# Linear attention and an MLP mixer in one kernel: attention on quarters of the PE array, u summed onto x in PSUM, pair 0 scaled in another order

## The chip, the cores and the metric

The kernel runs on one NeuronCore of a Trainium2 chip. Its engines work from queues of their own: TensorE (PE; its weight loads are listed as PEld), VectorE (DVE), ScalarE (ACT), GpSimd (POOL) and SyncE (SP), which issues most of the DMAs. The metric is the device time of one execution in microseconds. A profile's span is a little shorter than that time: 811.9 against 813.68 us for the profiled execution.

## The reference

Everything is float32. q, k, v have the shape (8, 8, 576, 64): batch, heads, sequence, head dimension.

```python
kv = np.einsum('bhsd,bhse->bhde', k, v)
out = np.einsum('bhsd,bhde->bhse', q, kv)
rms = np.sqrt(np.mean(out * out, axis=-1, keepdims=True) + 1e-06)
x = (out / rms * g_norm)                       # then (B, S, H*D) = (8, 576, 512)
h = np.maximum(x.transpose(0, 2, 1) @ w_tok1, 0.0) @ w_tok2
u = x + h.transpose(0, 2, 1)
out = u + np.maximum(u @ w_ch1, 0.0) @ w_ch2
```

w_tok1 is 576 x 256, w_tok2 256 x 576, w_ch1 512 x 1536, w_ch2 1536 x 512; the four weights arrive in 64 bits and are rounded to 32 by the kernel.

## The kernel before

There are two passes. The second (from 204.85 us on) computes the channel mixing with a Strassen scheme and is not touched. The first makes u for all eight batches and stores it to DRAM. It works on four pairs of batches; in a pair, "side" is the batch. 576 tokens are four blocks of 128 and a rest of 64, and the rests of both sides share one block, so a pair has nine blocks of x (0 to 8), held in tiles X of two blocks: chunk c of 0 to 3 is two blocks of one side, chunk 4 the rest.

The steps of a pair have short names, and the order of all engines' work is written out by hand as lists of these names (`start` for the first pair's attention, `middle`, `steady` twice, `last`). `play` runs the list, and every instruction keeps its program order on its engine. A number n in a list puts n steps of the rounding of w_ch1 and w_ch2 there (one on ACT, six on DVE a block). The mixing of pair n runs together with the attention of pair n + 1.

- `kv` s h: half h (four heads) of k^T v for side s, 20 matmuls of 128 rows by 64 columns, the two heads of a pair of heads going to the two column halves of the array. They write the diagonal blocks of `kv_ps[half]`, one of two PSUM tiles that were zeroed at the start (line 1010).
- `e` s h: the eviction to `kvp[side]`, 128 x 256 with the zero blocks in it; on DVE in pair 0, on ACT afterwards.
- `a` c t: attention for 128 tokens and all heads: four matmuls (`attend`, line 355), one for each pair of heads, into one bank of `ps["o"]`, which has two. Each matmul is two records in the trace[...].
- `g`, `q`, `t` c t: gain (DVE: x = out * g), square (ACT) and total (DVE: mean square by head). `m`, `r`, `i`: mean, square root (ACT) and inverse for a group of chunks.
- `s` c t: scaling of x by the inverse, eight ACT instructions (line 424); `p` c t: the same as one POOL instruction (line 428).
- `h` s t and `hr`: the first token product, 128 x 512 outputs in the four banks of `ps["h"]`, then four relus on ACT. In pair 0 `h01` is cut by blocks (`h010` to `h013`).
- `u` i: the second token product for block i into a bank of `ps["h"]`, then on DVE (line 480) the sum with x, which is stored with every second block.
- `l`, `lq`: the loads of k, v and q on SP's queue; `j` n: n matmuls of an identity, before the first data come.

In the lists, `e00` of a steady pair stands behind `s30` and `s31` of the list before:

```python
"u6 t30 t31 m2 r2 1 i2 p20 p21 s30", f"u7 1 s31 {n1}", "u8 2"]        # a steady list ends
"kv00 l00 e00 1 -s40", "h00 3", "kv01 l01 e01 1", "h01 3", ...        # the next begins
```

`-s40` is a step of the pair before. [...]two banks for `o`, four for `h`, and two tiles for `kv`.

## Time and profile before

| what | us |
|---|---|
| median of 3 runs (813.6 to 814.11) | 813.75 |
| profiled execution, its span | 811.9 |
| first pass, start to last token product | 204.85 |
| PE busy, whole span | 796.3 |
| DVE busy | 690.8 |
| ACT busy | 288.2 |
| POOL busy | 79.9 |

Busy time is a union over instructions: 98% for PE says that it nearly always had something in flight, not that a stage couldn't be shorter. A row of the groups reads: line, engine, operation, output<-inputs, shapes, count, then busy us and mean ns of one, then the idle time before them and what ended it. In the timeline the columns are start, length, engine and instruction, with idle time before it in brackets.

### The profile page before, as it was taken

Reading aid. Unit: us, or ns where it says so; the run is one execution under the profiler, and the core shown is the slowest. Engines: PE = TensorE matmul, PEld = TensorE weight load, DVE = VectorE, ACT = ScalarE, POOL = GpSimd, SP = SyncE. Lnnn points to the kernel's source line nnn. Section 1 sums busy time; section 2 is a strip of 40 time slices with the busy share of each in tenths; the row PEclk is TensorE's granted clock in tenths of the full one; section 3 lists DMA queues with packets and bytes.
Section 4 is the critical chain, followed back from the end, with each engine's and each line's share of the span. In section 5 each row is a group of like instructions: output and inputs, shape, how many; then the busy total and the mean of one; then the engine's idle time right before and its main releaser. Section 6 shows DMA issues by size and latency. Waiting matters only on the chain.

```text
span 811.9 us, 16377 instructions
## 1 busy us (share of the span) xinstructions
PE 796.3 (98%) x6388; PEld 704.9 (87%) x6388; DVE 690.8 (85%) x1318; ACT 288.2 (35%) x805; POOL 79.9 (10%) x75
## 2 busy tenths in 40 slices
PE   6999999999999999999999999999999999999997
PEld 6655565543888899999999999999999999999996
DVE  4688989999986978988997997897898899799687
ACT  1355566471120134243234233333424323423331
POOL 1210101010000011003003003001100200300300
PEclk9999999999999999999999999999999999999999
DMA  9999998335458477368558638737836855764642
GB/s 294 324 342 329 341 357 290 131 130 169 166 203 294 169 213 244 131 210 256 174 182 247 211 134 270 238 118 249 268 123 213 249 178 190 239 199 136 202 147 82
DMA packets 97341, 175.43 MB, mean 216 GB/s; under 512 B 7024, under 2 KB 54128, under 8 KB 97264
## 3 DMA queue, kind: packets, MB, share of 16 engines
q1 hardware_dynamic: 95584, 172.65, 65.4%
q10 hardware_dynamic: 1680, 1.74, 0.7%
q8 instruction: 50, 0.82, 0.4%
q14 instruction: 27, 0.22, 0.1%
HBM read 137.79 MB, written 36.57 MB: 215 GB/s over the span
## 4 chain that ended last, share of the span: by engine, by line
PE 88%; DVE 7%; DMA 3%; issue 1%; ACT 0%; SPq 0%; ACTq 0%; DVEq 0%
PE ps_a L127 37%; PE ps_b L127 18%; PE ps_c L127 9%; PE ps_u L127 5%; PE ps_h L127 5%; PE ps_v L127 4%; PE ps_w L127 4%; PE ps_o L127 2%; DMA v_in<-in_v_dram 2%; PE ps_kv L127 2%; DMA k_in<-in_k_dram 1%; DVE w_ch L174 1%; DVE ms L399 1%; DVE w_ch L118 1%; DVE part L187 1%
## 5 line engine op out<-in xcount | busy, mean ns | idle before, releaser
L118 POOL TENSOR_TENSOR v<-v,v 128x384 f32<-128x384 f32 (+1 forms) x48 | 61.4, 1301 | 534.0 <-ACT v L124 494.0
L124 ACT COPY u<-ps_a 128x128 f32<-128x128 f32 (+1 forms) x160 | 56.1, 351 | 156.9 <-PE ps_a L127 156.9
L127 PE MATMUL ps_b<-uT,sums 128*128 128x128 f32 x672 | 86.2, 276 | 0.0
L127 PEld LDWEIGHTS ps_b<-uT,sums 128*128 128x128 f32 x672 | 80.7, 192 | 0.2
L118 DVE TENSOR_TENSOR v<-v,v 128x768 f32<-128x768 f32 (+1 forms) x86 | 79.4, 930 | 1.1
L127 PE MATMUL ps_a<-uT,w_ch 128*128 128x128 f32 x576 | 78.9, 275 | 0.0
L124 ACT COPY ps_c<-ps_a 128x128 f32<-128x128 f32 (+1 forms) x80 | 26.9, 336 | 130.1 <-PE ps_a L127 130.1
L118 DVE TENSOR_TENSOR v<-ps_b,u 128x384 f32<-128x384 f32 x112 | 61.4, 548 | 12.8 <-PE ps_b L127 11.0
L127 PEld LDWEIGHTS ps_a<-uT,w_ch 128*128 128x128 f32 x576 | 71.5, 192 | 0.4
L127 PE MATMUL ps_u<-h,w_tok 128*128 128x512 f32 (+1 forms) x160 | 66.9, 602 | 0.5 <-DVE x L118 0.5
L127 PE MATMUL ps_h<-x,w_tok 128*128 128x512 f32 (+1 forms) x160 | 65.8, 603 | 0.0
L118 DVE TENSOR_TENSOR uT<-uT 128x512 f32<-128x512 f32 (+4 forms) x103 | 63.0, 628 | 0.8
L127 PE MATMUL ps_a<-uT,w 128*128 128x128 f32 x432 | 60.0, 275 | 0.0
L127 PEld LDWEIGHTS ps_a<-uT,w 128*128 128x128 f32 x432 | 54.0, 192 | 0.0
L127 PEld LDWEIGHTS ps_h<-x,w_tok 128*128 128x128 f32 (+1 forms) x160 | 25.9, 189 | 31.1 <-issue 28.3
L118 DVE TENSOR_TENSOR xg<-xg,r 128x512 f32<-128x512 f32 (+1 forms) x78 | 50.8, 663 | 2.3 <-ACT r L124 1.6
L127 PEld LDWEIGHTS ps_u<-h,w_tok 128*128 128x128 f32 (+1 forms) x160 | 24.7, 179 | 30.2 <-issue 22.6
L121 ACT ACTIVATE v<-v 128x384 f32<-128x384 f32 (+1 forms) x86 | 42.6, 528 | 22.8 <-DVE v L118 22.4
L118 DVE TENSOR_TENSOR sv<-v 128x384 f32<-128x384 f32 x80 | 43.3, 549 | 8.4 <-ACT v L121 8.4
L424 ACT ACTIVATE x<-x,inv 128x64 f32<-128x64 f32 x184 | 46.0, 335 | 9.5 <-DVE inv L419 8.1
L127 PE MATMUL ps_a<-sums,sv 128*128 128x128 f32 x336 | 47.0, 276 | 0.0
L127 PE MATMUL ps_a<-uT,sums 128*128 128x128 f32 x336 | 46.8, 276 | 0.0
(128 smaller groups left out, 1589.2 us busy)
## 6 DMA issues: line engine op xcount, KB each, us to landing
sums<-sums SPq DMA_DIRECT2D x112, 576.0 KB, 4.2
qT<-in_q_dram SPq DMA_DIRECT2D x8, 1152.0 KB, 10.1
xt<-u_dram SPq DMA_DIRECT2D x36, 256.0 KB, 3.5
blocks<-y SPq DMA_DIRECT2D x72, 128.0 KB, 2.6
uT<-blocks SPq DMA_DIRECT2D x36, 256.0 KB, 5.2
xg<-u_dram SPq DMA_DIRECT2D x18, 512.0 KB, 4.9
k_in<-in_k_dram SPq DMA_DIRECT2D x16, 512.0 KB, 9.4
u_dram<-x SPq DMA_DIRECT2D x16, 512.0 KB, 3.9
```

The costliest lines, as they stand in the source:

```text
L118: keep(engine.tensor_tensor(out=o, in0=a, in1=b, op=op))
L121: keep(nc.scalar.activation(o, a, AF.Relu))
L124: keep(nc.scalar.copy(o, a))
L127: keep(nc.tensor.matmul(*a, **kw))
L174: keep(nc.vector.scalar_tensor_tensor(out=bits, in0=raw()[..., 1], scalar=0x80000000, in1=bits, op0=ALU.bitwise_and, op1=ALU.bitwise_or))
L187: keep(nc.vector.scalar_tensor_tensor(out=part[0], in0=raw()[..., 0], scalar=2.0 ** -52, in1=part[0], op0=ALU.mult, op1=ALU.mult))
L399: keep(nc.vector.tensor_reduce(stats_of(c)[0][:, ts(t, H)], sq[c, t], axis=AX.X, op=ALU.add))
L424: keep(nc.scalar.activation(x[:, i], x[:, i], AF.Copy, scale=inv[:, i]))
```

## The change

Attention is computed by quarters of the array: a matmul takes one head (64 rows) and 64 tokens (64 columns), so that a step `a` c now makes both blocks of a chunk, with 64 matmul records on four 64 x 64 tiles. The two heads of a pair go to different banks (`bank[c, h]` in place of `bank[c, t]`), so gain, square and total work by (chunk, head parity), and square of one bank stands beside gain of the other. `kvp` and `kv_ps` lose their zero blocks. `ps["o"]` has three banks, and the kv results one rotating tile in place of two fixed ones.

For some blocks x is copied into the PSUM bank ahead (`z` i, on ACT), the token product is added onto it, and u is copied back by ACT: six of nine blocks in pairs 0 to 2, all in pair 3. The other blocks keep the DVE sum.

In pair 0, `p01 p11 p21 p31` (POOL) become `s01 s11 s21 s31` (ACT) and `s10` becomes `p10`; the first token product is cut by blocks for both t, and the last warming matmuls (`j6`, `j2`) go.

```diff
-          for n, b in (("o", 2), ("kv", 1), ("h", 4))}
+          for n, b in (("o", 3), ("kv", 1), ("h", 4))}
...
-    kvp = [inp.tile([P, HP, P], F32, name=f"kvp{i}") for i in range(2)]
+    kvp = [inp.tile([P, HP, D], F32, name=f"kvp{i}") for i in range(2)]
...
+            o = kv_ps[side, half] = ps["kv"].tile([P, 2, D], F32, name="ps_kv")
...
-                        matmul(kv_ps[half][r, i, r], lhsT=kk[:, j, ds(i * P + h * D, D)],
-                               rhs=vv[:, j, ds(i * P + h * D, D)],
+                        at = ds(i * P + h * D, D)
+                        matmul(o[ds(h * D, D), i], lhsT=kk[:, j, at], rhs=vv[:, j, at],
...
-        def attend(c, t):
+        def attend(c):
+            o = [ps["o"].tile([P, 2, HP, D], F32, name="ps_o", tag="o") for _ in range(2)]
             side = c // 2
-            o = bank[c, t] = ps["o"].tile([P, DM], F32, name="ps_o", tag="o")
-            for hp in range(HP):
-                matmul(o[:, ts(hp, P)], lhsT=qT[2 * pair + side][:, hp, ts(2 * (c % 2) + t, P)],
-                       rhs=kvp[side][:, hp], start=True, stop=True)
+            for t in range(2):
+                for hp in range(HP):
+                    for n in range(2):
+                        for h in range(2):
+                            r = ds(h * D, D)
+                            matmul(o[h][ds(n * HF, HF), t, hp],
+                                   lhsT=qT[2 * pair + side][r, hp, ds((2 * (c % 2) + t) * P + n * HF, HF)],
+                                   rhs=kvp[side][r, hp], start=True, stop=True)
+            for h in range(2):
+                bank[c, h] = o[h].rearrange("p t k d -> p (t k) d")
...
+            x = X[pair, c].rearrange("p t (k h d) -> p (t k) h d", h=2, d=D)[:, :, h]
+            keep(nc.vector.tensor_mul(x, bank[c, h], g_sb.to_broadcast([P, number(c), D])))
...
+        def seed(i):
+            acc[i] = ps["h"].tile([P, DM], F32, name="ps_u", tag="h")
+            copy(acc[i], x_of(pair, i))
+
         def tok2(i):
...
+            first = i not in seeds
...
-                                     start=(t == 0), stop=(t == NTOK - 1))
+                           start=(first and t == 0), stop=(t == NTOK - 1), skip_group_check=True)
...
-            tensor_add(x, acc_u, x)
+            if first:
+                tensor_add(x, acc[i], x)
+            else:
+                copy(x, acc[i])
...
-    kv_ps = [ps["kv"].tile([P, 2, P], F32, name=f"ps_kv{i}") for i in range(2)]
-    for t in kv_ps:
-        keep(nc.vector.memset(t, 0.0))
...
+        "a0 q00 g01 q01 g00 t00 t01 m0 r0", "a1 g11 q10 i0 g10 q11 p00 s01 t10 t11 m1 r1",
+        "kv10 e10 i1 p10 s11", "h000 h001", "kv11 e11", "h002 h003",
+        "a2 q20 g21 q21 g20 t20 t21 m2 r2", "h010 h011", "a3 g31 q30 i2 g30 q31 p20 s21 t30 t31 m3 r3",
+        "h012", "a4 i3 p30 s31 q40 g41 q41 g40 t40 t41 m4 r4", "h013 w21 i4 s40 lq0 l10 l11"]
...
+        "h11 f2 w42 w43 w44", "hr w45 w46 w47 f3 z0", "a0 q00 g01 q01 g00 z1 t00 t01", "u0 1", "u1 1",
+        "a1 q10 g11 q11 g10 z3 t10 t11 m0 r0", "u2 i0 1", "kv10 e10 s00", "u3 z4 1 s01", "kv11 e11 1",
+        "u4 1", "a2 q20 g21 q21 g20 z6 s10", "u5 t20 t21 2", "a4 q40 g41 q41 g40 z7 lq0 l10 l11", "u6 t40 t41 2",
+        "a3 q30 g31 q31 g30 lq1 s11", "u7 t30 t31 m2 r2 1 i2 p20 p21 s30", "u8 1 s31"]
...
+            "kv00 l00 e00 1 -s40", "h00 3", "kv01 l01 e01 1", "h01 3", f"a0 q00 g01 q01 g00 {n0}",
+            "h10 1 t00 t01 2", "h11 4", "hr 2 z0 z1", "a1 q10 g11 q11 g10 1", "kv10 l10 e10 t10 t11 m0 r0 1",
+            "u0 i0 1", "kv11 l11 e11 z3", "u1 1 s00", "u2 z4 1", "a2 q20 g21 q21 g20 s01", "u3 t20 t21",
+            "u4 1 z6", "a4 q40 g41 q41 g40 lq0 s10", "u5 t40 t41 1", "a3 q30 g31 q31 g30 z7 lq1 s11",
+            "u6 t30 t31 m2 r2 1 i2 p20 p21 s30", f"u7 1 s31 {n1}", "u8 2"]
...
+    mixings = [token_mixing(p, (0, 1, 3, 4, 6, 7) if p < B // 2 - 1 else range(9)) for p in range(B // 2)]
...
+        "h00 c0 2 -s40 2", "h01 c1 2", "h10 c2 2", "h11 c3 2", "hr 1 z0 z1 z2 z3", "u0 z4 1", "u1 z5 1", "u2 z6",
+        "u3 z7 1", "u4 z8 1", "u5 1", "u6 1", "u7 c4", "u8"]
```

## The prediction

> **What bounds the kernel now.** I read the page first, then busy time by stretches of the first pass, the chain that ended last, and last the in-order queues of PE and ACT around the attention steps.

> ```profile
> PE 796.3 (98%) x6388; PEld 704.9 (87%) x6388; DVE 690.8 (85%) x1318; ACT 288.2 (35%) x805; POOL 79.9 (10%) x75
> ```

> PE is nearly full, ACT seems nearly idle. But the change touches the first pass alone (0 to 204.85 us). I cut it where "hr", the last token product, ends (100.74, 146.45) and where a pair begins or ends:

> ```profile
> 80.33:100.74 20.41, 20.41 (x139) 10.83 (x135) 19.57 (x30) 12.09 (x39) 2.76 (x2) 1.00 1.08 343
> 100.74:126.04 25.30, 25.30 (x186) 15.24 (x186) 21.97 (x42) 15.97 (x48) 0.00 (x0) 1.00 1.06 357
> 172.41:204.85 32.44, 31.92 (x82) 13.08 (x80) 32.16 (x40) 10.12 (x30) 3.03 (x2) 1.00 0.49 155
> ```

> Columns: stretch, then busy time of PE, weight load, DVE, ACT, POOL; clock, DMA share, GB/s. A pair takes 45.7 us, PE never pauses, and DVE is nearly as full. ACT is busy 16.0 of the 25.3 us in which u is made: that stretch, and not 35%, is what counts. The chain prices PE's blocks (start, length):

> ```profile
> 59.19 1.72 PE ps_u L127 x4
> 60.90 1.32 PE ps_kv L127 x40
> 62.22 1.91 PE ps_u L127 x4
> 110.97 1.78 PE ps_o L127 x16
> 116.19 1.02 PE ps_r L127 x16
> ```

> An attention chunk costs 1.78. The kv block is already in two column halves: 40 records in 1.32, about 0.06 a pair of records. The four ps_u records after it take 1.91 instead of 1.72, which shows what a change of tiling costs. The ACT queue at a pair's beginning:

> ```profile
> 83.18 2.02 ACT L424 ACTIVATE x<-x,inv 128x64 f32<-128x64 f32 x8 [1.38 <-DVE inv L419]
> 85.10 0.91 ACT L163 ACTIVATE w_ch<-raw 128x768 f32<-128x768 f32 x1
> 85.92 2.00 ACT L424 ACTIVATE x<-x,inv 128x64 f32<-128x64 f32 x8
> 87.83 0.35 ACT L124 COPY kvp<-ps_kv 128x256 f32<-128x256 f32 x1
> ```

> The eviction e00 of kv00 runs at 87.83, although kv00 had left PE at 81.6: it stands behind both scalings. And PE had run kv01 in between:

> ```profile
> 85.22 1.39 PE L127 MATMUL ps_kv<-v_in,k_in 128*64 128x64 f32 x40
> 86.54 3.70 PE L127 MATMUL ps_h<-x,w_tok 128*128 128x512 f32 x8
> ```

> It could, because kv_ps is two tiles. So today this lateness costs nothing.

> [...]no run shows four quarters at once. [...]the list of waits has ACT's sq waiting for DVE's x 41.4 us in 24 waits.[...]

> **The change, part by part.**

> *Quarters.* A chunk's 16 records become 64, of 64 columns. If four overlap, 16 fours at 0.06 are 0.96, plus about 0.35 for entering and leaving the mode (0.19 from the ps_u rows, the rest an estimate from the kv block's own ends): 1.31 against 1.78, a gain of 0.47; 0.82 where the block already stood between two changes of mode (a1 after hr, before kv10); ps_r 1.02 to about 0.6. A steady pair: 3 x 0.47 + 0.82 + 0.42 = 2.6 us of PE. Bounds: if only two overlap, 32 x 0.06 + 0.35 = 2.27, a loss of 0.5 a chunk[...]. I take 0.47.

> *u on x.* 27 adds leave DVE (678 ns each, about 18 us); 27 seeds and 27 copies come to ACT:

> ```profile
> L118 DVE TENSOR_TENSOR x<-ps_u,x 128x512 f32<-128x512 f32 x36 | 24.2, 678 | 5.7 <-PE ps_u L127 5.7
> L124 ACT COPY r<-ps_v 128x512 f32<-128x512 f32 x3 | 1.8, 587 | 21.2 <-PE ps_v L127 21.2
> ```

> A copy is 587 ns, in a row about 0.55 (three relus of 598 take 1.57). Seeds write PSUM from SBUF, which no row has at this size: 0.45 to 0.7, I take 0.55. Six seeds and six copies are 6.6 us in a stretch where ACT had 9.3 us free. DVE's relief is worth only what PE waits for DVE: 0.5 to 0.8 us at 195. The u stores on SP now follow ACT's copy; u7's copy comes about where DVE's add had come (83.1), so the loads behind them hardly move.

> *PSUM.* ps_o goes from 2 to 3 banks, kv from two tiles to one rotating one. So kv01 must wait for e00, and kv11 for e10. That is the new wait, and what is queued behind kv01 is all of PE.

> *The rest.* Four evictions a pair shrink from 356 to about 266 ns (the 128x128 copy): counted. Squares and gains keep their sizes; a4's in two halves add about 0.3 us to DVE, hidden in its relief. The two memsets at 0.9 us are hidden by the first loads, till 6.1. In pair 0, three scalings of 1.0 us move from POOL to ACT at 2.0 each.

> **Sum by stages**, against the span.

> *Steady pair*, T = end of hr:

> ```profile
> 100.84 1.57 ACT L121 ACTIVATE h<-ps_h 128x512 f32<-128x512 f32 x3 [0.26 <-PE ps_h L127]
> 102.29 0.94 ACT L163 ACTIVATE w_ch<-raw 128x768 f32<-128x768 f32 x1
> 130.37 0.92 ACT L163 ACTIVATE w_ch<-raw 128x768 f32<-128x768 f32 x1
> 131.19 0.34 ACT L124 COPY kvp<-ps_kv 128x256 f32<-128x256 f32 x1
> ```

> ACT: relus and a weight step to 2.5, z0 3.05, z1 3.6, q10 and q11 4.8, e10 5.1. PE would be ready for u0 at 2.3 but waits for z0: 3.1, against 3.3 before, so a1's gain is mostly gone; kv11 waits for e10 at 5.1, as late as before. r0 must wait for g10 (after q10), two totals and the mean on DVE, till 6.9: ACT stands 1.8 us. Then, ends: u0's copy 7.7, e11 7.9, z3 8.5, u1's copy 9.05, s00 11.05, z4 11.6, weight step 12.5, a2's squares 13.7, s01 15.7, copies of u3, u4 and z6 17.4, a4's squares 18.1, s10 20.1, a3's squares 21.5, z7 22.05, s11 24.05, u6's copy 24.6, r2 24.85, wait for the inverse on DVE 26.1, s30 28.1, u7's copy 28.65, s31 30.65, weight step 31.6, e00 31.9. PE meanwhile waits for u3's bank and z7, and is ready for kv01 at 30.6. kv01 thus starts at 31.95; before it was 30.2 (130.94 - 100.74). +1.75, less a0's 0.47: +1.3.

> *Middle pair*, the same way: from the end of a3 its squares 1.25, s11 3.25, u7's copy 3.85, r2 4.1, inverse 5.4, s30 7.4, weight step 8.3, s31 10.3, e00 10.6. PE reaches kv01 8.5 after a3 (76.75 to 85.22). A stand of 2.1; with the quarters' gain and two old waits for ps_o on one side, and z0 and z4 on the other, I get kv01 at +1.85 and, less a0, +1.4.

> *Start.* Attention of side 1 can't begin before its q has landed: issued at 18.8, up to 10.9 us to landing, 29.75. From there a3 ends near 34.2, s21 runs to 37.9, s31 (POOL had p31) waits for the inverse to 39.2 and runs to 41.2, only then a4's squares, its root, s40 (44.1 to 46.1), e00 46.3. Middle's kv01 was at 44.85: +1.5, though kv00 may start 2.1 earlier (its v was issued at 26.2, up to 11.2 us to landing, so about 37.5; it ran at 39.9).

> *Last steady stretch* (to 172.41): no kv follows; -0.2. *Last mixing:*

> ```profile
> 188.26 7.13 PE L127 MATMUL ps_u<-h,w_tok 128*128 128x512 f32 x16
> 195.92 9.00 PE L127 MATMUL ps_u<-h,w_tok 128*128 128x512 f32 x24 [0.52 <-DVE x L118]
> ```

> u0 began at 188.26 with hr; now it waits for the relus (1.7 after hr) and z0: +2.3, and the wait for DVE goes, -0.8: +1.5.

> Sum: 1.5 + 1.4 + 1.3 - 0.2 + 1.5 = +5.5. Span 811.9 + 5.5 = 817.4. The profiled run was 813.68, the runs' median 813.75: 1.85 over the span. **819.2 us.**

> **Rivals.**

> *1. PE keeps the pace (other side).* Speaking for it: ACT's busy sum from the first relu to e00 is 29.4 us, below 30.2, so without dependency waits the copies fit. Against: those waits (1.8 for r0, 1.3 for the inverse) come out of chains that exist now. It decides from e00 at about T + 29, 2.9 us earlier than my chain. Then start -2.1 (its v), middle -3.6 (2.6 and 1.0 of old waits), two steady stretches -2.6 each, last +1.5: -9.4, 804.3; with some waits left, 808.

> *2. Only two quarters overlap.* For: the trace shows pairs alone. Against: in kv the two halves cost no more than one. Each chunk is then 0.96 dearer than in my sum; on the path lies a0, the others partly behind ACT, some 1.5 us a pair: 825.

> *3. Both even out:* half of rival 1's gain against half the stands: 813.7.

> **How the numbers follow.** Likeliest (ACT paces, e00 holds kv01): 0.52, own range 816 to 823. Rival 1: 0.30, 803 to 812. Rival 2: 0.10. Rival 3: 0.08. A change under 0.2% (1.6 us) can't be told from none here. So slower 0.62, same 0.08, faster 0.30. The range 806 to 824 leaves out the best of rival 1 and most of rival 2.

> **What will show it.** Right: PE waiting at kv01 for ACT kvp, 1 to 3 us, three times; at u0 of the last pair for ACT ps_u about 2 us; chunks of 64 records in about 1.0; ACT over 22 us busy in the u stretch. Wrong: kv01 directly behind its h00 or h10 block, or a chunk of about 2.2. I would be wrong if seeds were much cheaper than 0.55, or if a lighter DVE brought m0 and m2 so early that ACT never stands.

## The result and the profile after

The changed kernel takes 824.58 us (824.21 to 825.17, 4 runs) against 813.93 us of the kernel before in the same session: ratio 1.0132, 95% interval 1.0114 to 1.0149, slower by 10.65 us. Forecast were 819.2 us and a range of 806 to 824: the sign is right, the size is not, and the time lies 0.6 us outside the range.

The page of the changed kernel, its line of busy times:

```profile
PE 788.7 (96%) x7204; PEld 690.4 (84%) x7204; DVE 675.0 (82%) x1297; ACT 319.5 (39%) x887; POOL 77.2 (9%) x72
```

The span is 822.9 us, 11.0 more than before, although TensorE is busy 7.6 us less. So it stands idle 18.6 us more (34.2 against 15.6), and, as will be seen, some of its busy time is slower too. The stretches that answer to those shown of before (columns as there):

```profile
85.10:109.13 24.03, 21.67 (x186) 10.58 (x183) 18.61 (x28) 11.30 (x36) 2.79 (x2) 0.93 1.08 340
109.13:134.15 25.02, 23.35 (x346) 12.34 (x346) 19.75 (x39) 20.64 (x60) 0.00 (x0) 1.00 0.96 306
180.69:216.25 35.56, 33.41 (x82) 13.75 (x80) 29.76 (x35) 20.26 (x48) 3.22 (x2) 0.95 0.45 144
```

In the middle line ACT's work rises from 15.97 to 20.64 us, as was to be expected. The last number but two of the first and third line is new: TensorE's granted clock, 1.00 before, is 0.93 and 0.95. The chain of the changed kernel at a pair's beginning:

```profile
87.49 2.02 ACT x L438 x8
89.51 0.79 ACT w_ch L163
90.30 1.91 ACT x L438 x8
92.21 0.16 ACT kvp L124
92.37 0.04 issue
92.42 1.39 PE ps_kv L127 x40
93.80 5.33 PE ps_h L127 x8
```

It is the ACT queue of before, two scalings with a weight step between and then e00, but now it stands on the chain, and kv01 begins behind it at 92.42. (Before, kv01 ran at 85.22 beside it.) The last line is the surprise: the eight ps_h records that took 3.70 us before take 5.33. The list of waits in the first 220 us has TensorE's largest on ScalarE (total us, times, longest):

```profile
PE ps_u L127 <- ACT ps_u L124: 7.5, 7, 2.1
PE ps_kv L127 <- ACT kvp L124: 7.4, 4, 3.7
PE ps_o L127 <- ACT sq L396: 2.7, 2, 1.4
```

Three pauses at kv01 hold most of the second line: 3.75, 2.36 and 0.64 us. The longest of the first line, 2.15 us, is at u0 of the last pair. Now the stretches around the three long pauses. They are cut every 3.41 us; the column before the last two is the granted clock.

```profile
46.15:49.56 3.41, 1.44 (x41) 1.38 (x42) 2.56 (x7) 2.56 (x11) 0.00 (x0) 1.00 1.11 305
49.56:52.97 3.41, 3.41 (x5) 1.33 (x6) 3.24 (x7) 0.91 (x2) 0.00 (x0) 0.50 1.13 305
52.97:56.38 3.41, 3.41 (x13) 1.24 (x11) 3.19 (x5) 0.46 (x1) 0.00 (x0) 1.00 1.04 363
90.52:93.93 3.41, 1.51 (x41) 1.45 (x42) 3.27 (x6) 3.41 (x16) 0.00 (x0) 1.00 1.10 303
93.93:97.34 3.41, 3.41 (x5) 1.35 (x5) 2.28 (x3) 1.30 (x4) 0.00 (x0) 0.50 1.06 389
...
196.33:199.74 3.41, 1.26 (x5) 0.51 (x4) 3.41 (x5) 3.15 (x8) 0.00 (x0) 1.00 0.52 152
199.74:203.15 3.41, 3.41 (x6) 1.34 (x5) 3.31 (x5) 1.68 (x3) 0.00 (x0) 0.50 0.60 154
```

After a stretch in which TensorE was busy 1.26 to 1.51 of 3.41 us, its granted clock is 0.50 in the whole next stretch, and 1.00 again from 52.97, 97.34 and 203.15 on. The half-clock stretches start at 49.56, 93.93 and 199.74, which are 13.0 and 31.0 times 3.413 apart; I call the stretches of this grid windows. As an estimate, 3.41 x 0.5 = 1.7 us are lost each time, three times: 5.1 us that no step of the forecast held. The mean clocks of the other three runs, 0.990 to 0.992, are no higher than the 0.993 of this one.

### The profile page after: what moved, and what is told of

Same layout as the page of the kernel before. It is cut to its first block, busy times and chain, and to the rows that moved or that the text cites. A ratio compares the mean times of both kernels' runs of the same rounds, so it can differ in the third digit from the quotient of the medians.

```text
span 822.9 us, 18063 instructions
## 1 busy us (share of the span) xinstructions
PE 788.7 (96%) x7204; PEld 690.4 (84%) x7204; DVE 675.0 (82%) x1297; ACT 319.5 (39%) x887; POOL 77.2 (9%) x72
## 4 chain that ended last, share of the span: by engine, by line
PE 86%; DVE 6%; ACT 5%; issue 1%; DMA 1%; ACTq 0%; POOL 0%; SPq 0%; DVEq 0%
PE ps_a L127 36%; PE ps_b L127 18%; PE ps_c L127 9%; PE ps_h L127 6%; PE ps_u L127 5%; PE ps_v L127 4%; PE ps_w L127 4%; ACT x L438 3%; PE ps_kv L127 1%; PE ps_o L127 1%; DVE x L392 1%; DMA raw<-in_moe_w_tok_dram 1%; DVE ms L412 1%; ACT h L121 0%; ACT sq L396 0%
## 5 line engine op out<-in xcount | busy, mean ns | idle before, releaser
L124 ACT COPY u<-ps_a 128x128 f32<-128x128 f32 (+1 forms) x160 | 56.0, 350 | 156.6 <-PE ps_a L127 156.6
L118 POOL TENSOR_TENSOR v<-v,v 128x384 f32<-128x384 f32 (+1 forms) x48 | 61.4, 1300 | 536.8 <-ACT v L124 497.0
L127 PE MATMUL ps_b<-uT,sums 128*128 128x128 f32 x672 | 86.2, 276 | 0.0
L127 PEld LDWEIGHTS ps_b<-uT,sums 128*128 128x128 f32 x672 | 80.7, 192 | 0.2
L118 DVE TENSOR_TENSOR v<-v,v 128x768 f32<-128x768 f32 (+1 forms) x86 | 79.4, 931 | 1.1
L127 PE MATMUL ps_a<-uT,w_ch 128*128 128x128 f32 x576 | 78.8, 275 | 0.0
L124 ACT COPY ps_c<-ps_a 128x128 f32<-128x128 f32 (+1 forms) x80 | 26.9, 336 | 130.1 <-PE ps_a L127 130.1
L127 PE MATMUL ps_u<-h,w_tok 128*128 128x512 f32 (+1 forms) x160 | 69.4, 619 | 7.5 <-ACT ps_u L124 7.5
L127 PEld LDWEIGHTS ps_a<-uT,w_ch 128*128 128x128 f32 x576 | 71.5, 192 | 0.4
L118 DVE TENSOR_TENSOR v<-ps_b,u 128x384 f32<-128x384 f32 x112 | 61.5, 549 | 12.5 <-PE ps_b L127 10.7
L127 PE MATMUL ps_h<-x,w_tok 128*128 128x512 f32 (+1 forms) x160 | 69.8, 629 | 1.5 <-POOL x L443 1.5
L118 DVE TENSOR_TENSOR uT<-uT 128x512 f32<-128x512 f32 (+4 forms) x103 | 63.0, 628 | 0.8
L127 PE MATMUL ps_a<-uT,w 128*128 128x128 f32 x432 | 60.0, 275 | 0.0
L127 PEld LDWEIGHTS ps_u<-h,w_tok 128*128 128x128 f32 (+1 forms) x160 | 25.2, 182 | 38.9 <-issue 26.2
L127 PEld LDWEIGHTS ps_h<-x,w_tok 128*128 128x128 f32 (+1 forms) x160 | 27.0, 196 | 36.3 <-issue 29.9
L438 ACT ACTIVATE x<-x,inv 128x64 f32<-128x64 f32 x208 | 52.5, 339 | 8.4 <-DVE inv L431 8.4
L127 PEld LDWEIGHTS ps_a<-uT,w 128*128 128x128 f32 x432 | 54.0, 192 | 0.0
L118 DVE TENSOR_TENSOR xg<-xg,r 128x512 f32<-128x512 f32 (+1 forms) x78 | 50.9, 664 | 2.3 <-ACT r L124 1.6
L121 ACT ACTIVATE v<-v 128x384 f32<-128x384 f32 (+1 forms) x86 | 42.5, 528 | 23.0 <-DVE v L118 22.5
L118 DVE TENSOR_TENSOR sv<-v 128x384 f32<-128x384 f32 x80 | 43.3, 550 | 7.1 <-ACT v L121 7.1
L127 PE MATMUL ps_a<-sums,sv 128*128 128x128 f32 x336 | 47.0, 276 | 0.0
L127 PE MATMUL ps_a<-uT,sums 128*128 128x128 f32 x336 | 46.8, 275 | 0.0
```

The costliest lines, as they stand in the source:

```text
L118: keep(engine.tensor_tensor(out=o, in0=a, in1=b, op=op))
L121: keep(nc.scalar.activation(o, a, AF.Relu))
L124: keep(nc.scalar.copy(o, a))
L127: keep(nc.tensor.matmul(*a, **kw))
L438: keep(nc.scalar.activation(x[:, k, h], x[:, k, h], AF.Copy, scale=inv[:, h, k]))
```

## The experiments

Times are medians. Each kernel was timed beside the kernel before, whose median was 813.5 to 813.9 in every session, so I give the difference to it as well.

### Keep the clock up, leave the waits

Unused matmuls fill TensorE's three long waits (`y15` ahead of kv01 of the middle, `y10` in the first steady stage, `y9` ahead of the last u0):

```diff
+    def fill_wait(n):
+        o = ps["o"].tile([P, DM], F32, name="ps_w", tag="o")
+        for _ in range(n):
+            matmul(o[:, :P], lhsT=ident, rhs=ident, start=True, stop=True)
...
-"kv01 e01 l01 w41 w35 w36 w37"
+"y15 kv01 e01 l01 w41 w35 w36 w37"
```

> The changed kernel with unused 128x128 matmuls of the identity into a spare bank where TensorE waits longest: 15 ahead of kv01 in the middle stage, 10 ahead of kv01 in the first steady stage, 9 ahead of u0 of the last pair. The waits stay; only TensorE is busy in them. Theory A (half of the loss is the clock, halved for 3.4 us after each of the three pauses): the clock stays at 1.0 throughout and the time falls by about 5 us (3 x 1.7), to 818 to 821 us, while kv01 and u0 still start some 1 to 4 us late. Rival B (the clock record is beside the point; the records are slow for another reason, such as ScalarE still being behind): no change, 823 to 826 us.

819.75 us (+6.3 to before, 4.8 below the changed kernel). In its trace the granted clock is 1.00 throughout the first pass; around the first steady kv01:

```profile
88.00:90.00 2.00, 1.87 (x21) 1.68 (x20) 1.93 (x4) 2.00 (x10) 0.00 (x0) 1.00 1.08 311
90.00:92.00 2.00, 2.00 (x42) 1.57 (x41) 1.93 (x3) 2.00 (x10) 0.00 (x0) 1.00 1.06 327
92.00:94.00 2.00, 2.00 (x6) 0.93 (x5) 1.62 (x3) 0.66 (x1) 0.00 (x0) 1.00 1.05 396
```

Matmuls that compute nothing made the kernel faster by nearly the three half-clock stretches. So the clock is shown to be 4.4 to 4.8 of the 10.65 us, a little under half. The spans of the four runs are now 817.3 to 818.4; the forecast's sum of the waits alone was 817.4.

Shorter fills in the same places (9, 4 and 3 matmuls):

> The changed kernel with unused matmuls in the same three waits of TensorE, but fewer: 9, 4 and 3 instead of 15, 10 and 9 (0.22 us each, so about 2.0, 0.9 and 0.7 us of pauses of 3.75, 2.36 and 2.15). Theory A (the clock is judged in fixed windows of 3.41 us; a pause halves it only where it takes more than about 1.88 us of one window, the smallest seen with a half clock in the traces so far, against 1.86 without): the pauses left, 1.8 us at most, halve it nowhere, and the time is that of the fully filled waits, 818 to 821 us, though three pauses of 1.4 to 1.8 us stay. Rival B (any pause of more than a microsecond near these places halves the clock, and filling helps only in proportion): one to three half-clock stretches stay, 821 to 824.5 us.

819.78 us (+6.0). Pauses of 1.46 and 1.28 us stay at the steady kv01 and at u0, and the clock stays at 1.00 behind both. One half-clock stretch came elsewhere, at 37.83, after a stretch of the first stage with quarter matmuls and a pause of 1.31 us (of the kind shown in the next section), in which PE was busy 1.94 of 3.41 us. So the fill needn't be complete, but 1.88 us of pause isn't a rule for every mix of work.

### The key-value bank

The change's one bank for kv alone, put into the kernel before (the freed bank goes to the attention results):

```diff
-          for n, b in (("o", 2), ("kv", 1), ("h", 4))}
+          for n, b in (("o", 3), ("kv", 1), ("h", 4))}
...
-    kv_ps = [ps["kv"].tile([P, 2, P], F32, name=f"ps_kv{i}") for i in range(2)]
+    kv_ps = [ps["kv"].tile([P, 2, P], F32, name="ps_kv")] * 2
```

> The kernel before the change, with one key-value bank that both halves share (memset once), and the freed bank given to the attention results (three instead of two). Nothing else is changed: no quarters, no seeding, scaling as before. Theory A (the single bank is the larger part of the loss): kv01 must wait for e00 in this kernel too; in the first steady stage, where ScalarE has two scalings of the pair before ahead of e00, by 2 to 3 us with or without a half-clock stretch; in the middle stage by about 1.5 us or less, since there GpSimd does the scaling. 816 to 821 us. Rival B (the bank alone costs nothing: kv01 came 5 us after kv00 in the kernel before, which is long enough for the eviction): 813 to 815 us.

820.31 us (+6.9). TensorE stands 3.93 us ahead of the first steady kv01 (it starts at 89.48, before at 85.22), with a half clock from 89.5 on, and 1.60 us ahead of the middle's. The wait named in the forecast exists without quarters and without seeding, and it is larger than was reckoned.

The other way, two kv banks in the changed kernel, at the cost of the third bank for attention results:

```diff
-(("o", 3), ("kv", 1), ("h", 4))
+(("o", 2), ("kv", 2), ("h", 4))
```

> The changed kernel with two PSUM banks for the key-value products and two for the attention results, instead of one and three. Theory A (the single key-value bank makes TensorE wait for ScalarE's eviction three times, 4.3, 2.9 and 1.2 us, and the two long pauses each halve TensorE's clock for 3.4 us, 1.7 us each): the waits of kv01 on ScalarE go, as do two of the three half-clock stretches; what stays is the pause and the half clock at the last pair's u0, and one attention chunk can no longer run ahead of its readers. 813 to 818 us. Rival B (the path simply moves to the next thing that ScalarE is late with, so that the pauses come back at h or u as large as they were): 822 to 825 us, pauses of the same sum at other places.

819.31 us (+5.9): between the two theories. The pauses at kv01 are gone. The longest pause after the first loads is now in the first stage. Work of TensorE and ScalarE there (start, length, work, idle before):

```profile
33.30 0.60 ACT L396 ACTIVATE sq<-ps_o 128x512 f32<-128x512 f32 x1 [0.17 <-DVE x L392]
34.28 1.15 PE L127 MATMUL ps_o<-kvp,qT 64*64 64x64 f32 x62
35.55 0.60 ACT L396 ACTIVATE sq<-ps_o 128x512 f32<-128x512 f32 x1
38.03 0.37 PE L127 MATMUL ps_o<-kvp,qT 64*64 64x64 f32 x2 [2.59 <-issue]
```

It looks like a wait for a result bank, since a chunk of quarters fills two and there are only two. The trace says otherwise. The last reader of the chunk before ends at 33.90, ahead of this chunk, and TensorE stands before the last two of its 64 records, when ScalarE already squares one of the two banks. "issue" means that the profile shows nothing that was waited for.

What the traces have at this place is a packet of q8, a queue that the page calls "instruction" (packets, MB, share). The first line is this kernel's and the changed kernel's, the second that of the kernel before:

```profile
q8 instruction: 57, 0.93, 0.5%
q8 instruction: 50, 0.82, 0.4%
```

The packets are of 16 KB. TensorE has 14,408 records of matmuls and weight loads in the first, 12,776 in the second: 253 and 256 for each packet, if all were its own. Here a packet runs from 35.58 to 36.73, and TensorE goes on 1.3 us after its end. A pause with "issue" stands at this place of a3 in all 13 kernels with quarters, 0.2 to 2.6 us long (1.67 in the changed kernel), and each time TensorE goes on 1.2 to 1.6 us after the end of such a packet; the three kernels without quarters have none there. A chunk is now 64 matmul and 64 weight-load records in 1.09 us, where 16 and 16 took 1.78. That TensorE waits for what the packet brings is my reading of these times; no run changed it alone, so the cause is not shown.

With the 2.59 us goes a half clock from 37.73 on for 6.8 us, which the changed kernel's 1.67 us didn't bring. Why the packet came later here is open. The last u0 keeps its 2.15 us and its half clock. So the second kv bank takes away the waits at kv01, and the time of this run holds a clock loss that comes from another pause.

Two half tiles in one kv bank were meant to have both:

```diff
-            o = kv_ps[side, half] = ps["kv"].tile([P, 2, D], F32, name="ps_kv")
+            o = kv_ps[side, half] = kv_bank[:, half]
```

> The changed kernel with both halves' key-value products in one PSUM bank, a half tile each (2 x 512 bytes a partition), so that kv01 needn't wait for the eviction of kv00, while the attention results keep their three banks. Theory A (the waits at kv01 are the single buffer's doing and nothing else stands behind them): the two pauses of 3.75 and 2.36 us and their half clocks go without the new pause of 2.6 us that the two-and-two division of the banks brought; left are the small pauses and the last u0 with its half clock: 814 to 818 us. Rival B ([...]kv01 waits all the same): 822 to 826 us.

824.51 us, the same as the changed kernel, with the pause of 3.76 us at kv01 still put down to ACT's kvp. The edit did not take the wait away, so it says nothing against the theory. Whether the order was kept because both halves lie in one bank, or only because they are one tile of the program, no run here separates.

### The place in ScalarE's queue

The first pair's scaling back on GpSimd in three of four places:

```diff
-"... g10 q11 p00 s01 ..."  "kv10 e10 i1 p10 s11"  "... p20 s21 ..."  "a4 i3 p30 s31 ..."
+"... g10 q11 p00 p01 ..."  "kv10 e10 i1 s10 p11"  "... p20 p21 ..."  "a4 i3 p30 p31 ..."
```

> The changed kernel with the first pair's scaling shared as before the change: p00 p01, s10 p11, p20 p21, p30 p31 instead of p00 s01, p10 s11, p20 s21, p30 s31, that is three of four ScalarE scalings of eight instructions (2 us each) given back to GpSimd. Theory A (e00 and so kv01 of the middle stage come late because s31, a square and s40 stand ahead of e00 in ScalarE's queue): kv01 of the middle starts some 2 to 3 us earlier and its half clock goes, 4 to 5 us in all: 819.5 to 821 us. Rival B ([...]r4 waits for VectorE's chain anyway, so that e00 isn't earlier): no change or slower, 824 to 827 us.

822.0 us (+8.5). Between the theories: kv01 of the middle comes 1.85 us earlier (46.27 against 48.12), but its pause is still 2.29 us and its half clock stays. What stands ahead of e00 then is s40. So this part is worth 2.1 to 2.6 us and isn't the main one.

e00 first at each change of pair, in the changed kernel with everything else in place:

```diff
-"kv00 e00 w31 ..."              "kv00 l00 e00 1 -s40"            "... p20 p21 s30", f"u7 1 s31 {n1}"
+"kv00 e00 -s40 w31 ..."         "kv00 l00 e00 -s30 -s31 1 -s40"  "... p20 p21", f"u7 1 {n1}"
```

> The changed kernel, seeding and all, with e00 first in ScalarE's queue at every change of pair (s40 of the first pair, s30 and s31 of the later ones issued after it). Theory A (two of the three long waits come from the order of ScalarE's queue, and their half clocks from the waits): kv01 of the middle starts 2 us earlier, that of the first steady stage 2.4 with no half clock, that of the second 0.6: 817 to 820 us. Rival B (the copies of the seeding fill the queue so that e00 is late in any place): 822 to 825 us.

817.12 us (+3.3), as A had it: the same scalings issued a few us later save 7.3 to 7.5 us. The steady kv01 follow TensorE's h00 at once; the middle's waits 1.08 us; no half clock is left in the first pass. The long wait at the last u0 is unchanged (2.15 us), and in this trace it fell across two windows and the clock stayed at 1.00: 1.7 us of the gain there, as an estimate, is luck, and not the order of the queue.

### The seeding

None in the changed kernel (`token_mixing(p, ())`, all z steps taken out of the lists):

> The changed kernel without the seeding: no copy of x into PSUM ahead, u is added to x on VectorE as before the change, in all four pairs. Quarters, single key-value bank and scaling as in the changed kernel. Theory A (the seeding costs at the last pair's u0, whose wait on the copies is 2.15 us and brings a half clock of 1.7 us, and it loads ScalarE in the steady stages, ahead of the evictions that TensorE waits for): that pause and its half clock go, the rest stays: 818 to 821 us. Rival B (VectorE is the engine that the stage can't do without, 27 additions of about 0.6 us more on it give back 5 us and more in the u stretches): 825 to 832 us.

816.62 us (+3.0), 8.0 below the changed kernel and better than the theory said. In its trace the pause of 2.62 us at the first steady kv01 is still there, but costs no clock, while one half-clock stretch came in the first stage, at 37.55. The seeding left out in the last pair only:

> The changed kernel with the seeding in the first three mixings only; in the last pair u is added to x on VectorE as before the change. Theory A (of the 8 us that the seeding costs in the changed kernel, some 3 to 4 lie in the last mixing, the wait at u0 and its half clock, and the rest in the u stretches of the middle and steady pairs, where the copies share ScalarE with the scalings): 820 to 822 us, and the last pair starts as late as in the changed kernel. Rival B (all of it lies in the last mixing): 816 to 818 us.

819.91 us (+6.1), just under A's range: 4.7 of the 8.0 lie in the last mixing (the pause at u0 with its half clock), 3.3 in the three pairs before. (The five runs without seeding spread over 2.9 us, so this split is good to about 1 us.) Seeding alone in the kernel before, the same 27 places, whole-row matmuls and two kv banks:

```diff
-            tensor_add(x, acc_u, x)
+            if first:
+                tensor_add(x, acc[i], x)
+            else:
+                copy(x, acc[i])
```

> The kernel before the change with the seeding alone: x copied into PSUM ahead of u in the same 27 places, u accumulated onto it, the sum copied back by ScalarE; whole-row matmuls, two key-value banks and the scaling as before. Theory A (the seeding by itself costs most of what it costs in the changed kernel, 8 us there: its long wait at the last u0 with a half clock, some 4 us, and the copies ahead of the evictions and squares on ScalarE in each of three earlier pairs, some 1 us each): 818 to 822 us. Rival B (the seeding costs only where the single key-value bank makes TensorE wait for ScalarE; with two banks it is nearly free but for the last u0): 813 to 817.5 us.

820.14 us (+6.4). The last mixing again has the pause of 2.15 us and a half clock; the last pair's h00 starts at 176.9 instead of 172.4, so 4.5 us are lost in the pairs before. The seeding loses on its own.

A mixed form, the shared kv tile above with u0 to u2 of the last pair unseeded:

```diff
-range(9)
+range(3, 9)
-"hr 1 z0 z1 z2 z3", "u0 z4 1"
+"hr 1 z3", "u0 z4 1"
```

> The kernel with the shared key-value bank, and in the last pair u0 to u2 not seeded (VectorE adds them to x as before), u3 to u8 seeded. Theory A (u0 of the last pair waits for ScalarE, which has the rectifications of h11 and hr and then the copies ahead; u0 to u2 unseeded start at once and give it the time): the last long pause and its half clock go, about 2 + 1.7 us less than with the shared bank alone: 810 to 814 us. Rival B (unseeded, u0 waits for a bank that the seeds hold, or u3 waits as u0 did): no less than with the shared bank alone, 814 to 818 us.

825.32 us (+11.7): theory A fell. u0 starts at once, but a later u stands longer, 3.12 us at 203.59. The chain there:

```profile
201.73 0.60 DVE x L118
202.33 0.60 DVE w_ch L170
202.93 0.61 DVE x L118
203.54 0.04 issue
203.59 11.83 PE ps_u L127 x23
```

The banks come free only when VectorE has added (TensorE's wait of 3.1 us is put down to DVE's x), and VectorE has rounding of weights and other work in its queue ahead. A wait on ScalarE became one on VectorE.

### Quarters alone

The changed kernel without seeding, with the scaling as before, and with the two half tiles in one kv bank (which alone had changed nothing):

> Quarters alone: the changed kernel with the shared key-value bank, without the seeding, and with the first pair's scaling shared with GpSimd as before the change. Theory A (the quarters save what was forecast, 0.8 us for each whole chunk and 0.4 for each rest, some 3 to 4 us a pair, and what the change lost came from the other three parts): 803 to 810 us, faster than the kernel before. Rival B (the quarters themselves cost it: their results come in another layout, which holds VectorE and ScalarE longer, so that TensorE waits for banks of the attention results): 813 to 820 us.

814.96 us (+1.3; ratio 1.0008, 0.9996 to 1.002): the same as before. The time is that of B, the reason is not: the kv01 waits that this kernel still has, 2.29 us with a half clock in the middle, 2.61 and 0.5 in the steady stages, and 1.6 at the last kv11, take back what the quarters gain; the last kernel of this section shows it. The pause of 2.61 us is worth a look:

```profile
85.30:88.71 3.41, 1.55 (x4) 0.38 (x2) 3.34 (x4) 3.41 (x14) 2.08 (x2) 1.00 1.11 297
88.71:92.13 3.42, 2.67 (x43) 1.92 (x44) 3.28 (x5) 3.42 (x14) 0.00 (x0) 1.00 1.07 343
```

It is longer than the 2.15 us at u0 that a half clock followed, and the clock stays at 1.00. It lies across two windows, in which TensorE is busy 1.55 and 2.67 us; at the changed kernel's u0 it was busy 1.26 us of one.

The twelve runs of this one program also show what the clock costs, without any edit: the five with a mean clock of 0.999 or 1.000 took 812.8 to 813.6 us, the seven with 0.989 to 0.997 took 814.9 to 816.6. Whether the pauses fall in other places of the windows from run to run is not shown: only one run of each kernel has a trace.

With two kv banks and two result banks (and no seeding, scaling as before):

> Quarters with the banks as before the change: two key-value banks and two banks of attention results, no seeding, the first pair's scaling shared with GpSimd. Theory A (the quarters gain what was forecast, and two result banks are enough since VectorE and ScalarE read the results within about 2 us): 804 to 809 us. Rival B (a chunk of quarters fills both banks, so that the next chunk waits until VectorE and ScalarE have read both; in the first stage, where nothing lies between the chunks, that makes a long wait and a half clock): 809 to 815 us.

812.03 us (-1.8; ratio 0.9979, 0.997 to 0.9988), the time of B, and in part its reason. TensorE waits 6.0 us for ACT's squares of the result banks, against 3.9 in the next kernel with three banks. But the pause of 1.88 us in a3 of the first pair, with half clock from 38.05 to 44.9, is no wait for banks: it is the pause of "issue" again, and ends 1.31 us after a packet of q8.

With one kv bank (a rotating tile again), three result banks and e00 first:

> The changed kernel without seeding, with the first pair's scaling shared with GpSimd as before the change, and with e00 first in ScalarE's queue at every change of pair: s40 of the first pair, and s30 and s31 of each later pair, are issued after e00 and not ahead of it. One key-value bank and three result banks as in the changed kernel. Theory A (TensorE's waits at kv01 are the eviction's place in ScalarE's queue behind two scalings of 2 us each): against quarters alone (814.96 us) the waits of kv01 go, 2.3 us and its half clock of 1.7 in the middle, 2.6 and 0.6 in the steady stages: 806 to 809 us. Rival B (the scalings held back come late for h10 and the rectifications, and TensorE waits there instead): 812 to 816 us.

809.34 us (-4.4; ratio 0.9946, 0.9934 to 0.9959), slightly above A's range and faster than both kernels. ScalarE's timeline at the beginning of the first steady pair:

```profile
81.60 0.90 ACT L163 ACTIVATE w_ch<-raw 128x768 f32<-128x768 f32 x1
82.40 0.24 ACT L124 COPY kvp<-ps_kv 128x128 f32<-128x128 f32 x1
83.14 5.84 ACT L438 ACTIVATE x<-x,inv 128x64 f32<-128x64 f32 x24 [0.50 <-DVE inv L431]
```

and TensorE's:

```profile
80.47 1.33 PE L127 MATMUL ps_kv<-v_in,k_in 128*64 128x64 f32 x40
81.74 3.70 PE L127 MATMUL ps_h<-x,w_tok 128*128 128x512 f32 x8
85.37 1.39 PE L127 MATMUL ps_kv<-v_in,k_in 128*64 128x64 f32 x40
86.69 3.70 PE L127 MATMUL ps_h<-x,w_tok 128*128 128x512 f32 x8
```

The eviction leaves 5.84 us of scaling behind it instead of having it ahead; kv01 waits for nothing, and the block after it takes 3.70 us again. From kv00 of the first steady pair to kv00 of the next it is 42.99 us (80.47 to 123.46), 45.71 before: 2.7 us, where the forecast had 2.6 for the quarters. TensorE has no pause above 0.3 us in either stretch.

## Why the prediction was wrong in size

*Quarters: right in the steady pairs.* In the chain of the changed kernel:

```profile
119.10 1.09 PE ps_o L127 x64
120.20 3.63 PE ps_u L127 x8
123.83 0.62 PE ps_r L127 x32
```

A chunk is 1.09 us (forecast "about 1.0" for the records), the rest 0.62 (0.6). Rival 2, only two at once, is out.

*The new wait: right in place.* kv01 waits for kvp three times, u0 of the last pair for ps_u. The rival that TensorE keeps the pace fell by both.

*Sum by stages.* I measure what each stage adds between its ends in the two traces (the end of hr; h00 of the last pair; the first record of the second pass), and take 1.7 us off (3.41 x 0.5, an estimate) where a half-clock stretch lies in it:

| stage | forecast | measured | of it clock | left |
|---|---|---|---|---|
| start, to hr of the middle | +1.5 | +4.96 | 1.7 | +3.3 |
| middle, to hr of steady 1 | +1.4 | +3.43 | 1.7 | +1.7 |
| steady, to hr of steady 2 | +1.3 | -0.06 | 0 | -0.1 |
| last steady stretch | -0.2 | -0.05 | 0 | -0.1 |
| last mixing | +1.5 | +3.12 | 1.7 | +1.4 |
| second pass | 0 | -0.4 | 0 | -0.4 |
| sum | +5.5 | +11.0 | 5.1 | +5.8 |

Three steps failed. The first is the one that carries the time out of the range.

1. The missing term: the sum priced each wait at its own length, and put the clock at nothing. A wait of TensorE of 2.2 to 3.8 us cost up to 1.7 more through the clock, 5.1 in all. This alone puts the time outside the range (819.2 + 5.1 = 824.3), and the filled waits show it. In the three places 1.90 to 2.15 us without work inside one window (3.41 less the 1.51 to 1.26 busy) were followed by one at a clock of 0.50.

2. "Start", +1.5, was +3.3. The chain of the changed kernel:

```profile
34.32 1.67 issue
...
37.83 2.02 ACT x L438 x8
...
41.57 1.52 ACT x L438 x6
43.10 0.27 ACT sq L396
...
45.90 2.02 ACT x L438 x8
47.92 0.15 ACT kvp L124
48.07 0.04 issue
48.12 1.39 PE ps_kv L127 x40
```

a3 ended at 36.2, not 34.2. About 0.4 of this is q, which let a2 start at 30.16 and not 29.75; 1.67 is the pause of "issue" before a3's last record, shown above under the kv bank. The forecast priced the 64 records by their time in the array and put nothing for such a pause, which the kernel before, with 16 records, does not have there. All that stands behind keeps the delay: s31 ended at 43.1 (forecast 41.2), s40 at 47.9 (46.1), and kv01 began at 48.12 (46.35), 1.8 us late. What causes the pause is not shown, as said.

3. "Steady pair", +1.3, was -0.1. kv01 came 30.6 us after hr (139.76 - 109.13), not 31.95. A copy and seed were priced at 0.55 to 0.6 us; in the chains a row of them runs at 0.47 to 0.50. Over the twelve in this stretch that is about 1 us, as an estimate; the sign to look for, ACT busy over 22 us, was 20.64.

Errors 2 and 3 nearly cancel (+1.8 and -1.4), which is luck. With them cancelled, what is left without the clock, +5.8, looks like the forecast's +5.5. What the forecast didn't ask at all is how its four parts stand to each other: it had the quarters' gain (confirmed at 2.7 us a pair) used up by waits, and the runs show that most of those waits come from the order of a few ScalarE steps and from the seeding, not from the quarters.

## What to carry to other kernels

A pause of TensorE can have two prices. Here pauses of 2.15, 2.36 and 3.75 us cost their length and were each followed by 3.41 us at half clock, about 1.7 us more as an estimate, so look at the granted clock by stretches when pauses of about 2 us are forecast. When a double buffer becomes single, find the reader's place in its own in-order queue and move it ahead of work that nobody waits for yet: here that was worth 5.6 and 7.5 us in two kernels, and without the seeding, and with the first pair's scaling as before, a change that lost 10.65 us became one that gains 4.4. When a matmul is cut into smaller ones, look in the trace for new pauses as well as at the time of the records: a chunk here went from 1.78 to 1.09 us, and a3 of the first pair got a pause of 0.2 to 2.6 us. An engine at 35% isn't a free place for work if what it already does is waited for in order.
